# Residue-major layout for dilated attention, output stores from GpSimd's queue and a redone step order in an attention and feed-forward kernel

## The chip, the cores and the metric

The kernel runs on one core of one Trainium2 chip. The metric is the device time of one execution, in microseconds. A profile is taken from one execution of its own, and its span is a little shorter than the time of that execution (324.1 against 325.84 us for the kernel before). An execution is called slow when it takes over 1.5% longer than the fastest of the same kernel; ratios here use fast executions alone.

## The reference

Two stages follow one another: causal sliding attention, whose heads 4 to 7 are dilated by four, and a feed-forward pair with a leaky activation.

```python
B, H, S, D = 8, 8, 576, 64                      # attention; window 32, dilation 4
rel = pos[:, None] - pos[None, :]
mask_plain = (rel >= 0) & (rel < 32)                       # heads 0 to 3
mask_dil   = (rel >= 0) & (rel < 128) & (rel % 4 == 0)     # heads 4 to 7
attn = softmax(where(mask, q @ k.T / sqrt(D), -1e9));  x = attn @ v
x = x.transpose(0, 2, 1, 3).reshape(4608, 512)
h = x @ w_in                     # 512 -> 2048
out = maximum(0.01 * h, h) @ w_out   # 2048 -> 512, float32
```

## The kernel before

Everything is ordered by hand. A string, `PROGRAM`, is a list of steps, and each engine executes its share of them in that order. "Batch" n below is one half of the heads of one of the 8 batches: even n are the plain heads, odd n the dilated ones, so n runs from 0 to 15. A unit u is a third of a batch, n = u // 3.

| step | what it issues |
|---|---|
| `lq:n`, `gq:n`, `lv:n` | loads of q and k (from SyncE's queue, or as fp16 from GpSimd's), and of v |
| `lw:0:g`, `lw:1:g` | load quarter g of w_in, of w_out, from GpSimd's queue |
| `cq`, `cv` | casts of q or k, a copy inside v; the letter names the engine (V, P, A) |
| `T:n`, `B:n:p` | transposes of q and k, by DMA or on TensorE |
| `S:u`, `M:u`, `D:u` | scores and exp; mask; denominator, values and their product into `xT` |
| `I:c:j` | 4 matmuls of x @ w_in for chunk c, column block j; step I:c:j uses quarter j // 4 |
| `O:t:g` | 4 matmuls of g @ w_out for tile t of 128 tokens; after g = 3 the tile is stored |
| `Z:m` | m warm-up matmuls on zeros |

```python
PROGRAM = """
... cq:1:q:V:1 lw:0:0 ... lw:0:1 D:1:lp gq:2:b ... lw:0:2 B:3:1:VA M:5 lw:0:3 B:3:0:VA lv:2:b ...
gq:4:b S:11:m I:0:0 I:0:1 I:0:2 S:10:m ... I:0:7 I:0:8 S:7:m I:0:9 lw:1:2 ...
"""
# ... cut
    def transpose(n):
        for nm, dst in (("q", qT), ("k", kT)):
            o = dst[n % NB][:, -2 * S:].rearrange("p (c r) -> p c r", r=96)
            nc.sync.dma_start_transpose(o, qkh[n, nm][0:96, :])
# ... cut, in scores(u): kind is 1 for the dilated heads
                if kind:
                    ka = kT[n % NB][r, tok - 128 + j: tok - 128 + j + 4 * kp - 3: 4]
                    qa = qT[n % NB][r, tok - PAD + j: tok - PAD + j + 4 * w - 3: 4]
                else:
                    ka = kT[n % NB][r, tok + 96 * j - 32: tok + 96 * j + 96]
                    qa = qT[n % NB][r, tok - PAD + 96 * j: tok - PAD + 96 * j + 96]
                nc.tensor.matmul(sps[0:kp, hh, w * x:w * x + w], ka, qa, ...)
# ... cut
    def ff_out(t, g):
        if g == 0:
            ops[t] = psm.tile([128, 512], FP32, tag="pm", name="op")
        op = ops[t]
        g0 = 128 * t % GRING
        for j in range(4 * g, 4 * g + 4):
            nc.tensor.matmul(op, gt[:, j, g0:g0 + 128], w2[g][:, j % 4, :],
                             start=(j == 0), stop=(j == 15))
        if g == 3:
            ob = moe.tile([128, DM], FP32, tag="ob", bufs=2, name="ob")
            nc.scalar.copy(out=ob, in_=op)
            nc.scalar.dma_start(out[128 * t:128 * t + 128, :], ob)
            del ops[t]
```

The dilated heads read q and k transposed with a step of four columns, `ka` and `qa`. That step is what the first part of the change takes away.

The softmax here doesn't subtract the row's maximum and nothing guards it: scores larger than these inputs give would overflow.

## Time and profile before

| | before |
|---|---|
| time, median of three executions | 325.28 us (324.02 to 325.45) |
| span of the profile | 324.1 us |
| TensorE (PE) busy | 317.0 us, 98% |
| PE idle from 52 to 320 us | 0.00 us |
| step I:0:8 starts | 35.33 us |
| last matmul ends | 320.57 us |

The prediction shows the rows on which its argument rests. Three further rows of the page of the kernel before matter later. The first is the clock granted to PE in 40 equal slices, in tenths. The second counts DMA packets. The third is a group of instructions: line, engine, operation, operands and count, then busy us and mean ns of one, then idle time just before them and what ended most of it.

```profile
PEclk9999999999999999999999999999999999999999
DMA packets 111198, 42.38 MB, mean 131 GB/s; under 512 B 96832, under 2 KB 105024, under 8 KB 111168
...
L334 PE MATMUL hp<-xT,w 128*128 128x384 f16 (+1 forms) x832 | 140.9, 315 | 0.7 <-DMA w<-in_moe_w_in_dram 0.7
```

The clock never falls. All 832 matmuls of the first feed-forward product together waited 0.7 us, all of it for a quarter of w_in. So the start hangs on a load, but very little PE time is lost to it.

### The profile page before, as it was taken

To read this page: it belongs to the slowest core of one execution; us is meant where nothing else is said; L and a number is where in the kernel's file an instruction comes from. 1 tells how busy PE (TensorE), PEld (TensorE's weight loads), DVE (VectorE), ACT (ScalarE), POOL (GpSimd) and SP (SyncE) were. 2 spreads that over 40 slices of the span, in tenths; PEclk is the share of its full clock that TensorE was granted. 3 is DMA by queue.
4 is the path that set the end of the run, shared out by engine and by line. 5 is a ranking of instruction groups with operands and counts; after the bars stand their busy time and mean duration, and the time that the engine had idled before them with its cause. 6 is when DMAs were issued, how large, how long until landed. Compare 5 with 4: busy or idle time off the path is not lost.

```text
span 324.1 us, 6641 instructions
## 1 busy us (share of the span) xinstructions
PE 317.0 (98%) x2805; PEld 185.4 (57%) x2805; DVE 111.2 (34%) x166; ACT 191.8 (59%) x379; POOL 69.3 (21%) x92
## 2 busy tenths in 40 slices
PE   8998999999999999999999999999999999999995
PEld 3565585565756656656555565555665655565542
DVE  3473363203633084012353650454561530040000
ACT  1778696555756765936755773636856754464312
POOL 8751076033054220040310610200150000000000
PEclk9999999999999999999999999999999999999999
DMA  7999999969949931579899869303755000100003
GB/s 230 209 197 196 185 180 176 164 186 106 252 79 288 205 58 48 130 161 163 116 251 245 97 115 238 85 12 117 198 67 77 34 33 28 39 34 32 32 35 129
DMA packets 111198, 42.38 MB, mean 131 GB/s; under 512 B 96832, under 2 KB 105024, under 8 KB 111168
## 3 DMA queue, kind: packets, MB, share of 16 engines
q1 hardware_dynamic: 78240, 21.83, 34.2%
q0 software_dynamic: 27744, 10.68, 28.5%
q10 hardware_dynamic: 5184, 9.44, 7.9%
q8 instruction: 22, 0.36, 0.5%
q14 instruction: 8, 0.07, 0.1%
HBM read 36.70 MB, written 9.44 MB: 142 GB/s over the span
## 4 chain that ended last, share of the span: by engine, by line
PE 88%; DMA 9%; POOL 2%; ACT 0%; issue 0%; POOLq 0%
PE op L344 39%; PE hp L334 38%; DMA w<-in_moe_w_in_dram 5%; PE sps L261 5%; DMA vh<-in_v_dram 4%; PE den L287 3%; PE o L295 2%; PE tp L212 0%; POOL vh L169 0%; POOL vh L198 0%; POOL qh L183 0%; ACT ob L348 0%; POOL bias L106 0%; POOL bias L104 0%; POOL bias L103 0%
## 5 line engine op out<-in xcount | busy, mean ns | idle before, releaser
L334 PE MATMUL hp<-xT,w 128*128 128x384 f16 (+1 forms) x832 | 140.9, 315 | 0.7 <-DMA w<-in_moe_w_in_dram 0.7
L344 PE MATMUL op<-w,gt 128*128 128x512 f16 x576 | 137.0, 379 | 0.0
L336 ACT ACTIVATE gt<-hp 128x384 f16<-128x384 f32 (+1 forms) x208 | 93.0, 465 | 66.2 <-PE hp L334 63.8
L334 PEld LDWEIGHTS <-w 128*128 128x128 f16 x832 | 88.7, 114 | 43.9 <-issue 1.6
L344 PEld LDWEIGHTS <-gt 128*128 128x128 f16 x576 | 55.1, 98 | 57.2 <-issue 0.5
L312 DVE TENSOR_TENSOR xT<-o,rec 128x384 f16<-128x384 f32 (+1 forms) x64 | 33.6, 554 | 108.0 <-ACT rec L301 90.0
L303 DVE RECIPROCAL rec<-den 128x384 f32<-128x384 f32 x14 | 35.8, 2555 | 35.3 <-PE den L287 35.3
L264 ACT ACTIVATE er<-sps 128x768 f16<-128x768 f32 (+1 forms) x48 | 38.6, 804 | 10.7 <-PE sps L261 8.8
L348 ACT COPY ob<-op 128x512 f32<-128x512 f32 x36 | 21.1, 586 | 33.6 <-PE op L344 33.5
L186 POOL CAST kh<-kf 96x768 f16<-96x768 f32 x16 | 14.6, 936 | 106.3 <-DMA kf<-in_k_dram 81.2
L271 DVE TENSOR_TENSOR em<-er,mask 128x768 f16<-128x768 f16 (+1 forms) x44 | 25.4, 600 | 18.0 <-ACT er L264 17.8
L261 PE MATMUL sps<-qT,kT 64*128 64x96 f16 (+1 forms) x448 | 22.9, 229 | 0.0
L300 ACT ACTIVATE ln<-den 128x384 f32<-128x384 f32 x34 | 16.6, 488 | 8.7 <-PE den L287 8.1
L261 PEld LDWEIGHTS <-kT 64*128 64x128 f16 (+1 forms) x448 | 14.9, 121 | 10.2 <-issue 8.6
L301 ACT ACTIVATE rec<-ln 128x384 f32<-128x384 f32 x34 | 17.8, 524 | 1.1
L295 PEld LDWEIGHTS <-vh 128*64 128x64 f16 (+1 forms) x448 | 15.5, 110 | 2.4
L295 PE MATMUL o<-em,vh 128*64 128x96 f16 (+1 forms) x416 | 15.4, 201 | 0.0
L287 PE MATMUL den<-em,ones 128*64 128x384 f16 (+1 forms) x88 | 15.4, 346 | 0.0
L387 PE MATMUL wp<-xT 128*128 128x512 f16 x37 | 12.6, 455 | 1.5 <-DVE xT L113 1.3
L174 POOL DMA_DIRECT2D vh<-in_v_dram x16 | 10.0, 627 | 18.8 <-PE o L295 18.8
L195 POOL COPY vh<-vh 32x1472 f16<-32x1472 f16 x5 | 7.0, 1404 | 24.6 <-DMA vh<-in_v_dram 24.5
L287 PEld LDWEIGHTS <-ones 128*64 128x64 f16 (+1 forms) x96 | 5.3, 107 | 10.0 <-issue 8.3
(51 smaller groups left out, 97.8 us busy)
## 6 DMA issues: line engine op xcount, KB each, us to landing
out_dram<-ob ACTq DMA_DIRECT2D x36, 256.0 KB, 2.2
qf<-in_q_dram SPq DMA_DIRECT2D x11, 576.0 KB, 6.5
kf<-in_k_dram SPq DMA_DIRECT2D x11, 576.0 KB, 7.7
vh<-in_v_dram POOLq DMA_DIRECT2D x8, 288.0 KB, 7.5
w<-in_moe_w_in_dram POOLq DMA_DIRECT2D x4, 512.0 KB, 16.1
w<-in_moe_w_out_dram POOLq DMA_DIRECT2D x4, 512.0 KB, 11.1
vh<-in_v_dram POOLq DMA_DIRECT2D x8, 192.0 KB, 5.6
qf<-in_q_dram SPq DMA_DIRECT2D x4, 288.0 KB, 5.3
```

The lines of the kernel that those rows point to most:

```text
L261: nc.tensor.matmul(sps[0:kp, hh, w * x:w * x + w], ka, qa, start=not pe_mask, stop=not pe_mask or x == len(tiles) - 1)
L264: nc.scalar.activation(out=er[0:kp], in_=sps[0:kp, :, 0:384], func=AF.Exp, scale=SCALE)
L271: nc.vector.tensor_tensor(out=em[0:kp].rearrange("p h (t c) -> p h t c", c=w), in0=er[0:kp].rearrange("p h (t c) -> p h t c", c=w), in1=ba ...
L287: nc.tensor.matmul(den[64 * hh:64 * hh + 64, 0:384], ones[0:kp], em[0:kp, hh, :], start=True, stop=True)
L295: nc.tensor.matmul(o[64 * hh:64 * hh + 64, w * x:w * x + w], vt[0:kp, sl, :], em[0:kp, hh, w * x:w * x + w], start=True, stop=True)
L301: nc.scalar.activation(out=rec, in_=ln, func=AF.Exp, scale=-1.0)
L303: nc.vector.reciprocal(out=rec, in_=den[:, 0:384])
L312: nc.vector.tensor_tensor(out=out_x, in0=ins[0], in1=ins[1], op=ALU.mult)
L334: nc.tensor.matmul(hp[:, 0:w], w1[j // 4][:, i, j % 4::4], xT[:, i, x0:x0 + w], start=(i == 0), stop=(i == 3))
L336: nc.scalar.activation(out=gt[:, j, g0:g0 + w], in_=hp[:, 0:w], func=AF.Prelu, alpha=0.01)
L344: nc.tensor.matmul(op, gt[:, j, g0:g0 + 128], w2[g][:, j % 4, :], start=(j == 0), stop=(j == 15))
L348: nc.scalar.copy(out=ob, in_=op)
```

## The change

The change has five parts.

- **Residue-major**: q and k of the dilated batches 5, 7, ..., 15 are loaded, cast and transposed so that tokens of one residue modulo four are neighbours. The scores then read contiguous columns. It takes two transposes for each of q and k instead of one, four pieces of a cast instead of two, and larger tiles; the fp16 tiles get three buffers instead of four (`QHB`).
- **Stores**: four output buffers instead of two, and tiles 0 to 7 are stored from GpSimd's queue. The change was announced as moving most stores; its code moves 8 of 36.
- **Last tile in halves**: 16 matmuls, copy and store for columns 0 to 255, then the same for 256 to 511, so that the first store overlaps the second half.
- **Order**: the whole list of steps is new. It begins with the dilated batch 1, has 25 warm-up matmuls ahead of I:0:0 for 37, and loads the quarters of w_in as 0, 1, 3, 2.
- **No other arithmetic changes.**

```diff
-QHB = 4
+QHB = 3
 PROGRAM = """
-lq:0:0 Z:2 bias lq:0:1 lq:1:0 lq:1:1 lv:0:b Z:4 cq:0:q:P:0 cq:0:k:V:0 Z:9 lv:1:b B:0:0:AA cq:0:q:P:1
 ... (60 lines cut)
+Z:4 bias Z:3 lq:1:1 gq:3:b lv:1:b lv:0:b Z:2 cq:1:q:V:1 Z:5 gq:2:b lw:0:0 lw:0:1 cq:1:k:A:1 lw:0:3
+lw:0:2 B:1:1:AA lq:1:0 lv:3:b lq:0:0 lq:0:1 Z:2 cq:1:q:A:0 S:4:b cq:1:k:V:0 Z:3 B:1:0:VA cv:1:V:b
 ... (cut)
+D:5:lp S:11:m I:0:0 I:0:1 I:0:2 S:2:m I:0:3 I:0:4 I:0:5 M:2 lv:5:b I:0:6 I:0:7 S:9:m D:2:r I:0:8
 ... (cut)
+    if n >= NPE and n % 2:                                        # in load_qk
+        for a, i0, w in ((0, 0, 96), (1, 96, 48)):
+            nc.sync.dma_start(t[0:w, 16 * a:16 * a + 16, :].rearrange("p (h r) d -> p h (r d)", r=4),
+                              rows_ap(x, ((n // 2 * H + 4) * S + 4 * i0) * D,
+                                      [[4 * D, w], [S * D, 4], [1, 4 * D]]))
 ... (cast and transpose cut: four pieces, two transposes)
+                if kind and n >= NPE:                             # in scores
+                    c = S * p + 144 * j + (96 if s == 2 else 0)
+                    ka = kT[n % NB][r, PAD + c - 32: PAD + c - 32 + kp]
+                    qa = qT[n % NB][r, c: c + w]
 ... (cut)
+        last = t == NTOK // 128 - 1                               # in ff_out
+        if last and g < 3:
+            return
+        for c0, c1 in ((0, 256), (256, 512)) if last else ((0, 512),):
+            for j in range(0 if last else 4 * g, 4 * g + 4):
+                nc.tensor.matmul(op[:, c0:c1], gt[:, j, g0:g0 + 128], w2[j // 4][:, j % 4, c0:c1],
+                                 start=(j == 0), stop=(j == 15))
+            if g == 3:
+                ob = moe.tile([128, DM], FP32, tag="ob", bufs=4, name="ob")
+                nc.scalar.copy(out=ob[:, c0:c1], in_=op[:, c0:c1])
+                queue = nc.gpsimd if t < 8 else nc.scalar
+                queue.dma_start(out[128 * t:128 * t + 128, c0:c1], ob[:, c0:c1])
```

## The prediction

> **What bounds the kernel now.** I read the busy shares first, then the busy time of four stretches, then the chain of waits, then single groups. Page part 1, and the stretches from start to 36, 52, 320 and 325 us (columns: engine, busy us, instructions):
>
> ```profile
> PE 317.0 (98%) x2805; PEld 185.4 (57%) x2805; DVE 111.2 (34%) x166; ACT 191.8 (59%) x379; POOL 69.3 (21%) x92
> ...
> 0.00:36.00 36.00, 32.47 (x525) 17.95 (x525) 18.25 (x38) 22.24 (x38) 18.76 (x34) 1.00 1.18 206
> 36.00:52.00 16.00, 16.00 (x238) 12.17 (x238) 6.61 (x8) 13.43 (x33) 9.55 (x12) 1.00 1.23 186
> 52.00:320.00 268.00, 268.00 (x2047) 155.18 (x2042) 86.37 (x120) 155.59 (x308) 40.98 (x47) 1.00 0.62 118
> ```
>
> PE is busy 268.00 of 268.00 us from 52 us on, while ACT is at 58% and the DMA engines at 0.62. Ends of matmuls are modelled, so I ask the chain of waits (start us, length us, what) whether that is dense issue or long latency:
>
> ```profile
> 5.02 11.97 DMA vh<-in_v_dram
> 17.04 0.98 POOL vh L198
> 18.02 17.26 DMA w<-in_moe_w_in_dram
> 35.33 0.84 PE hp L334 x4
> 36.17 0.28 PE sps L261 x8
> 36.44 6.41 PE hp L334 x48
> ...
> 81.47 0.46 PE sps L261 x7
> 81.92 0.97 PE op L344 x4
> ...
> 83.55 0.71 PE sps L261 x16
> ...
> 167.29 0.97 PE op L344 x4
> ...
> 215.04 4.32 PE op L344 x20
> ```
>
> Here 20 `op` matmuls take 4.32 us, 0.216 each, and in the same view 20 `hp` matmuls take 3.25, 0.163 each: no holes. So there are two regimes. **Up to 35.3 us the chain is DMA**: the third quarter of w_in lands at 18.02+17.26 = 35.28, and step I:0:8, its first user, starts at 35.33. **From there PE itself is the chain**, with only attention between feed-forward matmuls. The last matmul ends at 320.57 (the final `ob` copy starts at 320.61), so PE needs 320.57-35.33 = **285.2 us after I:0:8**; 3.5 us of copy and store follow. Nothing on ACT, DVE, Pool or SP can shorten 285.2; only PE instructions that get cheaper, or an earlier 35.3.
>
> **What the Trainium skill says.** "TensorE: Matmul & The Clock Gate", Back-to-back issue gap, gives N/2.4+2.5 ns, 216 for N=512: the trace agrees (0.216). The same page, Weight-path perf modes, says that the fast weight load wants 128 weight columns: the trace fits it, score weight loads of 128 columns take 94 ns and those of 80 columns 168 (lines below). "Advanced Engine Details and Errata", SBUF Cachelines, wants two hits on a 16-byte line; a step of 4 fp16 values (8 bytes) has them, so by the page the dilated scores should cost nothing extra. The trace differs: eight contiguous score matmuls take 0.28 us of the chain, eight at step 4 take 0.46. I go by the trace. "DMA: Bandwidth & Descriptors", Issuing engines are not separate DMA queues, says that the issuing engine saves only sequencer time: I take that for the stores; no row of before tests it.
>
> The score lines, contiguous (window at 48.7), step 4 (81.3) and the 80x48 blocks (83.4); duration ns min/median/max:
>
> ```profile
> L261 PEld LDWEIGHTS <-kT x8: 92/94/96, 48.7 to 48.8; 64*128 64x128 f16 x8
> L261 PE MATMUL sps<-qT,kT x8: 202/203/213, 48.7 to 48.9; 64*128 64x96 f16 x8
> ...
> L261 PEld LDWEIGHTS <-kT x8: 108/113/132, 81.4 to 81.6; 64*128 64x128 f16 x8
> L261 PE MATMUL sps<-qT,kT x8: 252/264/270, 81.4 to 81.7; 64*128 64x96 f16 x8
> ...
> L261 PEld LDWEIGHTS <-kT x16: 147/168/170, 83.5 to 84.0; 64*80 64x80 f16 x16
> ```
>
> **The change, part by part.**
> 1. *Residue-major layout of dilated q and k (batches 5, 7, ..., 15; 1 and 3 keep step 4).* Six batches with two units of 8 matmuls: 12 x (0.46-0.28) = 2.2 us off PE. Six units of 16 blocks, 0.71 us each: with the step gone, eight pairs would take 0.28 to 0.35 us if the step caused all of it, and some 0.69 if the 80-column weight load is itself the limit. I take the middle, 0.53: 6 x 0.18 = 1.1 us (0.1 to 2.4). Sum **3.3 us on the path**. Around it: loads of 1 KB rows in place of 256 B, four transposes in place of two, four casts in place of two. A 96x768 cast takes 936 ns on Pool and 550 on DVE, both engines far from full; off the path.
> 2. *Order redone.* Each change between feed-forward, scores and values costs PE 0.10 us: `op x4` is 0.97 in the chain above just after attention against 0.86 inside a run. Counting changes in the two step lists from I:0:8 on: 116 before, 105 after, so **1.1 us less**. One score unit, S:10, moves from ahead of I:0:8 to behind it: +0.35.
> 3. *Last tile in halves.* 32 matmuls of 256 columns at about 0.109 instead of 16 at 0.216: +0.05. The last copy shrinks from 128x512 (586 ns) to 128x256; by the slope of the 128x384 and 128x192 `gt` activations (489 and 330 ns) that is 374 ns. The store behind it is half as large (2.0 to 2.2 us to landing now, mostly not size). **0.3 us less** after PE.
> 4. *Stores from Pool's queue, four buffers.* By the diff only tiles 0 to 7 of 36. It takes 8 x 0.338 us of issue off ACT, idle four tenths of the time; the `ob` copies wait for `op` (33.5 us), not for a buffer. Nothing on the path.
>
> From I:0:8 to the last matmul: 285.2-3.3-1.1+0.35+0.05 = **281.2 us**. Tail: 3.5-0.3 = 3.2.
>
> **The start decides the rest.** Pool's queue carries w_in. In the timeline its four loads are issued at 10.61, 13.16, 18.02 and 18.76 and land 14.2 (shortest) to 19.6 us (longest) later, so first at 24.8, last at 38.4. In those 13.6 us it also carries q and k of batch 2: three w blocks of 1.05 MB and 1.18 MB of q, k, 0.32 MB/us of source, 3.3 us a block. Before, I:0:8 needs the third block. After, the order on Pool is quarters 0, 1, **3, 2**, and I:0:8 reads quarter 2: the last block, with q, k of 2 now also ahead of all four. The same bytes lie before the last block as before, so it should land near 35.3+3.3 = 38.6. The loads are issued without Pool work between, but the queue was already full. PE has no more work ahead of I:0:8 than before, so it would reach it near 34 and wait four to five us. Fewer warm-up matmuls (25 for 37 ahead of I:0:0) cost nothing if DMA bounds the start.
>
> **Rivals.**
> - *A: the start is not later.* Something else delayed before's third block, or the first loads overlap better, and I:0:8 starts near 35.3: span 35.3+281.2+3.2 = 319.7. Measured time is 1.2 above the profiled span (325.28 against 324.1): 320.9. For it: before's order had almost no PE holes, so whoever ordered the steps knew this chip, and the new order should fit as well.
> - *B: the last block lands at 38.6:* 38.6+281.2+3.2+1.2 = 324.2. For it: the same bytes and the full DMA queues (1.18 to 1.23 of busy share, overlapping). Batch 6 is prefetched at 256 B rows and batch 5 follows it, one prefetch more than before's single batch 5 in this stretch, which could add one or two us. A hole of five us could also let PE's clock fall back; the warm-up matmuls at the start average 455 ns, not 379.
> - *C: a new wait inside the steady stretch.* Pool now holds its queue for stores, so casts and v loads behind them come later, and transposes wait. Against: Pool is 15% busy from 52 us on, and its `kh` casts wait 81 us for loads already. Each us of PE hole would add a us; I give it 10% for more than 2 us.
> - *D: a much earlier start.* To beat 2% (below 318.8) I:0:8 must start before 33.2 us, or the 80-column blocks must drop fully and the start gain a us. I see no removed byte that buys it.
>
> **Range and chances.** A and B at 0.45 and 0.55 give 0.45 x 320.9 + 0.55 x 324.2 = 322.7. The 80-column blocks swing 1.2 us either way, the start 2: 80% range 319.0 to 326.0. Faster by over 2% needs D: 0.09. Slower by over 2% (above 331.8) needs C badly: 0.03. Within 2%: 0.88.
>
> **What would show each step.** Score units of batches 5 and up at 0.28 us in the chain; 16-block units anywhere from 0.3 to 0.7 (this settles the weight-load question). PE from I:0:8 to the last matmul near 281. A `hp` wait on the DMA of `w` of some four us near 34 to 38 us says B; none says A. Batches 5 and up still at 0.46 would refute part 1; PE holes past 52 us behind `sps` or `vh` say C. The prediction is wrong above all if w's last block lands much before 36 or after 41 us.

## The result

The changed kernel takes 328.78 us (median of four, 327.14 to 329.16) against 325.01 (324.02 to 325.45) in the same rounds. The ratio is 1.0108, with a 95% interval of 1.0072 to 1.0144. Ratios in this document are the mean time of one kernel's fast executions over that of the other's of the same rounds, so not quite the ratio of the medians quoted. The kernel became about 1% slower. That is "same" at the 2% mark, the side that the prediction gave 0.88, but the time lies outside the predicted range of 319.0 to 326.0.

The profiled execution was the fastest one (327.14 us). The page of the changed kernel:

```profile
PE 312.5 (96%) x2811; PEld 186.0 (57%) x2811; DVE 111.4 (34%) x169; ACT 197.3 (61%) x389; POOL 79.8 (25%) x111
...
PEclk9987999999999999999999999999999999999999
...
DMA packets 90670, 42.38 MB, mean 130 GB/s; under 512 B 69776, under 2 KB 85136, under 8 KB 90640
```

PE works 4.5 us less than before (312.5 against 317.0) and the span is 1.3 us longer, so idle time took more than was saved. Not all of the 4.5 us is the layout: twelve warm-up matmuls are gone as well, and work at half clock counts double. The clock falls early on, in slices 3 and 4. There are a fifth fewer packets for the same bytes; the layout alone has as few (91038), so the longer rows of its loads make the difference. Next the same three stretches as before (columns: PE, PEld, DVE, ACT, POOL busy us, then clock, DMA share, GB/s):

```profile
0.00:36.00 36.00, 30.29 (x491) 18.09 (x493) 14.39 (x35) 21.34 (x37) 18.53 (x33) 0.91 1.17 208
36.00:52.00 16.00, 14.49 (x176) 11.04 (x170) 9.63 (x11) 11.57 (x29) 6.62 (x8) 1.00 1.31 225
52.00:320.00 268.00, 265.76 (x2142) 155.36 (x2135) 87.41 (x124) 163.99 (x324) 54.66 (x71) 1.00 0.62 116
```

PE now has 2.24 us of holes from 52 to 320 us, where it had none. (A hole in this document is the idle time that the timeline puts in brackets, unless it says otherwise.) The chain of waits of the changed kernel shows where its start comes from (start us, length us, what):

```profile
4.68 9.61 DMA vh<-in_v_dram
...
14.58 23.66 DMA w<-in_moe_w_in_dram
...
38.28 5.39 PE hp L355 x32
43.67 0.46 PE sps L282 x7
...
46.89 2.57 DVE rec L324
...
50.88 0.65 DVE qh L188
...
51.55 0.89 DVE qh L188 x2
...
53.05 0.33 DVE qh L188
...
53.80 1.56 DVE xT L333 x3
55.36 0.48 DVE em L292
...
55.88 0.35 PE den L308 x2
```

First, I:0:8 starts at 38.28, just after the last quarter of w_in landed at 14.58+23.66 = 38.24. This is rival B of the prediction. Second, the path then runs through VectorE from 46.9 to 55.8 us: a reciprocal, pieces of the cast of batch 5 (`qh`, 1.87 us together), products and a mask, and only then step D:6. PE stood still for 1.30 us in front of it. A cast that was to be off the path is on it.

The timeline of PE in the changed kernel shows the holes themselves; the bracket gives idle time before and what ended it:

```profile
20.63 0.23 PE L316 MATMUL o<-er,vh 128*64 128x96 f16 x1
22.95 0.53 PE L316 MATMUL o<-er,vh 128*64 128x96 f16 x7 [2.09 <-POOL vh L206]
...
36.45 0.34 PE L316 MATMUL o<-em,vh 128*64 128x96 f16 x8
38.28 3.93 PE L355 MATMUL hp<-xT,w 128*128 128x384 f16 x23 [1.50 <-DMA w<-in_moe_w_in_dram]
...
55.88 0.35 PE L308 MATMUL den<-em,ones 128*64 128x384 f16 x2 [1.30 <-DVE em L292]
```

PE waits 2.09 us for a copy inside v, and the records give it half the clock from 22.41 to 29.24 us. That delayed the work ahead of I:0:8, which is why only 1.50 us of hole is left in front of it here.

The score units of batches 5 and up, 16 blocks of 80x48, are the groups below (columns as in the prediction). In the chain such a unit takes 0.42 us, where it took 0.71 before.

```profile
L282 PEld LDWEIGHTS <-kT x16: 109/120/120, 118.5 to 118.8; 64*80 64x80 f16 x16
L282 PE MATMUL sps<-qT,kT x16: 192/193/213, 118.5 to 118.8; 64*80 64x48 f16 x16
...
118.61 0.42 PE sps L282 x16
```

Finally the end of the changed kernel, then that of the kernel before, from the timelines:

```profile
319.59 0.37 ACT L374 COPY ob<-op 128x256 f32<-128x256 f32 x1 [0.97 <-PE op L370]
...
320.01 1.91 PE L370 MATMUL op<-w,gt 128*128 128x256 f16 x16 [0.46 <-ACT ob L374]
321.96 0.37 ACT L374 COPY ob<-op 128x256 f32<-128x256 f32 x1 [2.00 <-PE op L370]
```

```profile
320.61 0.59 ACT L348 COPY ob<-op 128x512 f32<-128x512 f32 x1 [1.82 <-PE op L344]
```

The copy is shorter, 0.37 us for 0.59, but the second half of the matmuls waited until the copy of the first half was done. In the timeline it is ScalarE's copy (`ACT ob`) that ends its idle time of 0.46 us, and in the code both halves are one PSUM tile, `op`. From the last matmul to the end of the span it is 3.52 us, and was 3.57.

### The profile page after: what moved, and what is told of

Its sections match the earlier page's. It is cut to its first block, busy times and chain, and to the rows that moved or that the text cites. A ratio compares the mean times of both kernels' runs of the same rounds, so it can differ in the third digit from the quotient of the medians.

```text
span 325.4 us, 6728 instructions
## 1 busy us (share of the span) xinstructions
PE 312.5 (96%) x2811; PEld 186.0 (57%) x2811; DVE 111.4 (34%) x169; ACT 197.3 (61%) x389; POOL 79.8 (25%) x111
## 4 chain that ended last, share of the span: by engine, by line
PE 81%; DMA 10%; ACT 2%; DVE 2%; issue 2%; POOL 1%; POOLq 0%; DVEq 0%
PE op L370 37%; PE hp L355 36%; DMA w<-in_moe_w_in_dram 7%; PE sps L282 3%; DMA vh<-in_v_dram 3%; PE den L308 3%; PE o L316 2%; DVE rec L324 1%; ACT ln L321 1%; DVE xT L333 1%; ACT er L285 1%; DVE qh L188 1%; ACT rec L322 1%; PE tp L229 0%; DVE em L292 0%
## 5 line engine op out<-in xcount | busy, mean ns | idle before, releaser
L370 PE MATMUL op<-w,gt 128*128 128x512 f16 (+1 forms) x592 | 137.9, 373 | 0.5 <-ACT ob L374 0.5
L370 PEld LDWEIGHTS <-gt 128*128 128x128 f16 x592 | 56.6, 98 | 55.5 <-issue 0.6
L374 ACT COPY ob<-op 128x512 f32<-128x512 f32 (+1 forms) x37 | 21.2, 573 | 34.7 <-PE op L370 32.7
L292 DVE TENSOR_TENSOR em<-er,mask 128x768 f16<-128x768 f16 (+1 forms) x43 | 24.3, 587 | 22.5 <-ACT er L285 22.2
L282 PE MATMUL sps<-qT,kT 64*128 64x96 f16 (+1 forms) x448 | 19.1, 210 | 0.3
L206 POOL COPY vh<-vh 32x1472 f16<-32x1472 f16 x8 | 13.3, 1660 | 24.1 <-DMA vh<-in_v_dram 23.9
L282 PEld LDWEIGHTS <-kT 64*128 64x128 f16 (+1 forms) x448 | 12.4, 106 | 11.5 <-issue 9.1
L178 POOL DMA_DIRECT2D vh<-in_v_dram x16 | 10.1, 638 | 8.8 <-DMA vh<-in_v_dram 4.7
L197 POOL CAST kh<-kf 96x768 f16<-96x768 f32 x8 | 6.7, 879 | 20.6 <-DMA kf<-in_k_dram 20.6
L414 PE MATMUL wp<-xT 128*128 128x512 f16 x25 | 9.3, 480 | 1.5 <-DVE xT L112 1.3
L173 POOL DMA_DIRECT2D vh<-in_v_dram x8 | 9.6, 1204 | 3.9 <-PE hp L355 2.1
```

The costliest lines, as they stand in the source:

```text
L282: nc.tensor.matmul(sps[0:kp, hh, w * x:w * x + w], ka, qa, start=not pe_mask, stop=not pe_mask or x == len(tiles) - 1)
L292: nc.vector.tensor_tensor(out=em[0:kp].rearrange("p h (t c) -> p h t c", c=w), in0=er[0:kp].rearrange("p h (t c) -> p h t c", c=w), in1=ba ...
L370: nc.tensor.matmul(op[:, c0:c1], gt[:, j, g0:g0 + 128], w2[j // 4][:, j % 4, c0:c1], start=(j == 0), stop=(j == 15))
L374: nc.scalar.copy(out=ob[:, c0:c1], in_=op[:, c0:c1])
```

## The experiments

Fifteen kernels ran. All were timed in five rounds against the kernel before on the same chip, all gave correct results, and none changes what is computed. They ran in four calls, each on a chip of its own, so kernels of different calls are compared by their ratios to the kernel before. Each time is a median; "before" is the median of the kernel before in the same call.

**The theory**: exchanging the last two quarters of w_in puts the step I:0:8 behind the last load, and the hole there costs clock as well; the layout itself gains. **The rivals**: the layout costs more around it than it gains; the halves or the stores cost the time; the thin start with few warm-up matmuls is the cause; or the difference is scatter from execution to execution.

### Both kernels once more

`a_again` is the changed kernel and `b_again` the kernel before, without an edit.

> The changed kernel once more, to have a trace of its usual state and a time beside the variants of this group. The first trace was its fastest execution (327.14 us, granted clock 0.99); the others had 0.984 and 328.8. Theory 1 (a late quarter of w_in, holes after it, and a clock that falls in the holes): 328.5 us, ratio to the kernel before 1.011; I:0:8 starts when the last quarter lands, near 38.3 us; the clock is at half for some 10 us in two stretches instead of 6.8 us in one. Theory 2 (clock has no part, the first trace just differs): the extra 1.7 us then shows as PE holes at full clock.

> The kernel before itself, for a second trace. Theory 1 (its start moves by two us between executions with what the DMA engines do first, and PE's stretch after I:0:8 does not): ratio 1.000, I:0:8 between 33 and 36 us. Rival (the variants start earlier because of their edits): I:0:8 at 35.3 again.

The changed kernel took 328.16 us against 324.52, ratio 1.0106 (1.0087 to 1.0124). The kernel before against itself took 324.97 against 324.45, ratio 1.0008 (0.9987 to 1.0028). The loss is real. The second profile of the changed kernel has its clock fall in another place. Stretches of its span around I:0:8, columns as above:

```profile
34.50:38.00 3.50, 0.26 (x10) 0.12 (x6) 3.18 (x3) 0.66 (x1) 0.57 (x1) 1.00 1.22 239
38.00:42.20 4.20, 4.12 (x15) 2.14 (x16) 0.97 (x3) 1.47 (x3) 1.11 (x2) 0.59 1.17 239
42.20:46.00 3.80, 3.80 (x32) 2.57 (x31) 0.47 (x1) 2.77 (x6) 1.42 (x2) 1.00 1.73 216
```

This time PE was idle for 3.3 us ahead of I:0:8 (34.76 to 38.08), and then ran at half clock from 38.75 to 42.17. The four steps I:0:8 to I:0:11 took 4.3 us instead of 2.6, so the hole was followed by a second loss of 1.7 us. The 2.09 us wait for the copy inside v is in this profile too, from 21.00 to 23.09, but here the clock stayed full behind it. The start is where theory 1 had it; of its two slow stretches only one is there. In the executions of the first run the mean granted clock was 0.990 at 327.14 and 328.09 us, and 0.983 to 0.984 at 328.76 to 329.16; the kernel before has 0.998 to 1.000 in all 28 executions of these two tests. Only profiled executions show where in the span the clock fell.

The second profile of the kernel before corrects a reading of the first. Its chain of waits:

```profile
16.71 20.53 DMA w<-in_moe_w_in_dram
37.24 0.05 issue
37.29 4.44 PE hp L334 x36
```

Here the path goes through the fourth quarter, landed at 37.24, and I:0:12, which waited for it, while I:0:8 had started at 33.06. The last matmul ends 282.4 us after I:0:12 (319.67-37.29). In the first profile that is 282.2 (320.57-38.41), and the fourth quarter landed at 38.37 there. In the first trace both of the last quarters arrived just in time, and the prediction saw only the third. So in both traces I:0:12 starts as the *last* quarter lands, and the time from there on is the same. The start itself moves between executions, by 1.1 us here.

### The order of the quarters, in the changed kernel

```diff
- ... lw:0:1 cq:1:k:A:1 lw:0:3 lw:0:2 B:1:1:AA ...
+ ... lw:0:1 cq:1:k:A:1 lw:0:2 lw:0:3 B:1:1:AA ...
```

> The changed kernel with the quarters of w_in loaded in order 0,1,2,3 instead of 0,1,3,2. Theory 1 (I:0:8 is held by the block that lands last): quarter 2 lands one block earlier, near 34.5 us, I:0:8 to I:0:11 (2.6 us) run before quarter 3 is there, so 2 to 3 us less than the changed kernel, 325.5 to 326.5. Rival (the late start is hidden because PE is in any case behind, by D:0 and the slow clock): under 0.7 us.

It took 325.42 us against 324.52, ratio 1.0031 (0.9998 to 1.0065): 2.7 us of the loss go by this one exchange (2.4 us by the ratios), near the four steps of 0.65 us that it puts ahead of the last landing. Its executions spread from 323.39 us, with the clock at 1.000, to 327.38, with 0.988. The profiled one (327.05 us, clock 0.979) ran at half clock from 14.44 to 24.68 and from 55.40 to 58.81, the latter after PE had waited 1.93 us for a mask, ahead of D:6. So the exchange is the largest single part of the loss, and the other holes of the new order account for at least some of the rest.

### The order of the quarters, in the kernel before

```diff
- lw:0:2 B:3:1:VA M:5 lw:0:3 B:3:0:VA
+ lw:0:3 B:3:1:VA M:5 lw:0:2 B:3:0:VA
```

> The kernel before with only quarters 2 and 3 of w_in exchanged in the loading order. Theory 1 (the block that lands last holds I:0:8): I:0:8 starts near 38.4 instead of 35.3 and PE then idles for some 4 us ahead of it, after which its clock is at half for 3.4 us: 2.6 to 3 us for the wait and up to 1.7 for the clock, 327 to 329. Rival (the start has slack): within 0.7 us of before.

It took 329.72 us against 324.45, ratio 1.0154 (1.0128 to 1.0181). This exchange alone costs 5.0 us by the ratio, more than the whole change does and more than the 327 to 329 us expected. A second kernel fills the hole with warm-up matmuls, to separate waiting from clock:

```diff
- I:0:7 I:0:8
+ I:0:7 Z:15 I:0:8
```

> The kernel before with quarters 2 and 3 exchanged, and 15 warm-up matmuls (3.2 us) in the hole that this makes ahead of I:0:8. Theory 1 (of the 5.2 us that the exchange costs, the wait is some 3.3 and the fallen clock some 1.8): clock 1.0 from 6 us on, 3.2 to 3.7 us more than before, 327.8 to 328.2. Rival (the clock does not matter, all of it is the wait): 5 us more as without warm-ups, 329.7.

It took 327.92 us against 324.73, ratio 1.0101 (1.0072 to 1.0131). The stretches around I:0:8, without and then with the warm-up matmuls:

```profile
32.50:36.90 4.40, 0.39 (x3) 0.01 (x1) 0.88 (x2) 0.50 (x2) 0.00 (x0) 0.90 1.44 177
36.90:42.80 5.90, 5.87 (x25) 2.71 (x26) 0.56 (x1) 2.23 (x4) 2.88 (x4) 0.50 1.40 202
```

```profile
32.50:36.60 4.10, 3.74 (x19) 1.58 (x16) 1.00 (x2) 0.62 (x2) 0.00 (x0) 1.00 1.41 178
36.60:42.20 5.60, 5.58 (x40) 3.78 (x41) 0.56 (x1) 3.94 (x8) 2.57 (x3) 1.00 1.45 202
```

I:0:8 starts at nearly the same time, 36.93 and 36.62, in both when its quarter has landed. Behind it the clock is 0.50 in one and 1.00 in the other: in 5.9 us at half clock PE gets 25 matmuls done, in 5.6 us at full clock 40. Five of the six executions with the warm-up matmuls have a mean clock of 1.000, and the six without have 0.990 to 0.995. By the ratios, the exchange costs 1.01% (3.3 us) as a wait and another 0.53% (1.7 us, by the two intervals 0.4 to 3.0) as clock. The wait fits the steps that come to stand behind the last landing: in the first trace of the kernel before, I:0:8 to I:0:11 with a score unit between them take 3.1 us (35.33 to 38.41). Rival B of the prediction had 3.3 us for the wait; the clock it named and did not price.

### Warm-up matmuls in the changed kernel

```diff
- B:1:0:VA cv:1:V:b B:3:0:VA ... B:3:1:VV D:0:l ... D:2:r I:0:8
+ B:1:0:VA cv:1:V:b Z:4 B:3:0:VA ... B:3:1:VV Z:9 D:0:l ... D:2:r Z:7 I:0:8
```

> The changed kernel with 20 more warm-up matmuls in the three long holes of the start (4 ahead of B:3:0, 9 ahead of D:0, 7 ahead of I:0:8). Theory 1 (the holes let the clock fall, and in most executions the slow clock reaches work that bounds): granted clock 1.0 throughout from 6 us on, 1 to 2 us less than the changed kernel, 327. Rival (the start is bound by DMA, the clock does not matter): within 0.3 us.

It took 328.43 us against 324.52, ratio 1.0121 (1.0105 to 1.0136), and so missed. Two of the three fillers did what they should: the trace has full clock until 38.0. The third failed because a warm-up matmul writes the tile `den`, which step D:2 just ahead was still reading for its reciprocal. The seven matmuls came late, from 38 to 41 us, at half clock, and pushed I:0:8 to 40.92. So the run does not show what any of the three fillers is worth. It bears on the clock all the same: the slow stretch, from 38.00 to 41.41 us, fell almost wholly on warm-up matmuls, and from I:0:8 to the last matmul this kernel needs 282.8 us, where the second profile of the changed kernel needs 284.5.

### The last tile

```diff
-        last = t == NTOK // 128 - 1
+        last = False
```

> The changed kernel with the last tile computed and stored whole, as before. Theory 1 (the second half waits on ACT's copy of the first, 0.62 us of hole, and the store is not faster): 0.5 us less than the changed kernel. Rival (halving does help the tail, as predicted): 0.3 us more.

The changed kernel with its last tile whole took 326.79 us against 324.52, ratio 1.0065 (1.0053 to 1.0078). Halving therefore cost 1.4 us by the medians. The kernel before with the halves alone:

> The kernel before with the last tile in halves alone. Theory 1 (second half waits for ACT's copy of the first): a hole of 0.6 us between the halves, 0.3 us saved in copy and store, so 0.3 to 0.5 us more than before. Rival (halving helps as predicted, the hole belongs to the new order): 0.2 to 0.3 us less.

It took 325.09 us against 324.45, ratio 1.0020 (0.9994 to 1.0045), and the wait between the halves is in its timeline too:

```profile
317.79 1.91 PE L349 MATMUL op<-w,gt 128*128 128x256 f16 x16 [0.53 <-ACT ob L353]
```

In the changed kernel the tail behind the last matmul is 3.76 us with the tile whole and 3.52 with halves, so halving saves 0.24 there; in the kernel before it is 3.57 and 3.48. The matmuls lose 0.62 by the wait (from start to start, the step between the halves takes 0.73 us instead of 0.11) and 0.05 by their number. The traces thus account for some 0.4 us of loss, 0.6 in the kernel before. That the medians of the changed kernel differ by more is not explained. Its executions with the tile whole are within 0.8 us of one another although their mean clock runs from 0.982 to 1.000, so a fallen clock does not cost the same wherever it falls.

### The stores

```diff
-            nc.scalar.dma_start(out[128 * t:128 * t + 128, :], ob)
+            queue = nc.gpsimd if t < 8 else nc.scalar      # and four buffers
+            queue.dma_start(...)
```

> The kernel before with stores of tiles 0 to 7 from Pool's queue and four output buffers alone. Theory 1 (stores are off the path): within 0.4 us of before. Rival (Pool holds its queue behind the stores, casts and loads come late): holes ahead of sps or tp between 60 and 110 us, over 1 us more.

It took 325.05 us against 324.45, ratio 1.0014 (0.9987 to 1.0040): nothing.

### The layout alone

This is the kernel before, in its own order, with the new load, cast, transpose and scores (four fp16 buffers as before).

```diff
+                if kind and n >= NPE:      # and the load, cast and transpose of the change
+                    ka = kT[n % NB][r, PAD + c - 32: PAD + c - 32 + kp]
+                    qa = qT[n % NB][r, c: c + w]
```

> The kernel before with the residue-major layout of dilated q and k alone (loads, casts, transposes, scores of batches 5 to 15), old step order, four half buffers. Theory 1 (PE is the chain from I:0:8 on, so cheaper score matmuls come off the end one for one): per unit 0.46 to 0.28 us and, as the trace of the changed kernel has it, 0.72 to 0.42 for the 16-block units, 12 x 0.18 + 6 x 0.30 = 4.0 us less, 320.5, ratio 0.988. Rival (more DMA packets, casts and transposes come back as holes): under 2 us less, holes ahead of sps of odd batches.

It took 322.09 us against 324.45, ratio 0.9936 (0.9904 to 0.9967). The layout gains, but less than the 4.0 us that the score units promise. PE's busy time from I:0:8 to the last matmul, before and with the layout, shows 3.5 us:

```profile
35.33:320.57 285.24, 285.24 (x2284) 167.78 (x2284) 92.98 (x128) 169.02 (x340) 50.53 (x58) 1.00 0.66 122
...
32.80:316.53 283.73, 281.72 (x2286) 164.90 (x2283) 94.05 (x138) 169.56 (x345) 55.15 (x70) 1.00 0.69 122
```

And PE has 2.01 us of holes there, where it had none. The largest is one which the timeline explains:

```profile
66.90 0.58 ACT L375 COPY ob<-op 128x512 f32<-128x512 f32 x1 [4.18 <-DMA out_dram<-ob]
67.53 1.72 PE L356 MATMUL hp<-xT,w 128*128 128x384 f16 x8 [1.45 <-ACT ob L375]
```

ScalarE waited 4.18 us for an output buffer whose store was still under way, and PE waited for ScalarE. With two buffers, a store that takes longer while the new loads run holds up the matmuls. So I added one:

```diff
-            ob = moe.tile([128, DM], FP32, tag="ob", bufs=2, name="ob")
+            ob = moe.tile([128, DM], FP32, tag="ob", bufs=3, name="ob")    # ln: one buffer
```

> The kernel before with the residue-major layout and three output buffers instead of two (the scratch ln in one buffer to make room). In the trace with two buffers PE stood 1.8 us at 66 us: the output copy on ACT waited 4.2 us for an earlier store that was slow beside the new loads. Theory 1 (the missing 1.6 us of the 4.0 expected are such waits, most of it this one): that hole is gone, 1.5 us less than with two buffers, 320.6. Rival (another wait takes its place): within 0.5 us of it, 322.

Four output buffers and four fp16 buffers do not fit together: the build refuses them, with 6 KB a partition left where 8 are needed, and even three need `ln` cut to one. With three fp16 buffers it builds. That may be why the change has three; no run tests what they cost. It took 321.37 us against 324.73, ratio 0.9893 (0.9858 to 0.9929). One execution of 325.93 us counts as slow and is left out of the ratio; without it the median is 320.92. Its mean clock was 0.988, so it is of the kind that the changed kernel has all the time. **It beats both kernels.** Its stretch up to 316 us:

```profile
52.00:316.00 264.00, 263.06 (x2023) 151.36 (x2021) 85.78 (x127) 154.71 (x310) 42.51 (x52) 1.00 0.62 118
```

PE has 0.94 us of holes left there, the hole at 66 us is gone, and the clock stays up. So extra output buffers are not idle ballast, as the prediction took them to be: with the new layout a third one removes a wait. What that is worth is not clear of the noise: 0.9893 against 0.9936 is 1.4 us, as theory 1 had it, but the two intervals overlap and come from different chips. Nor is all of the gain on the kernel before the layout's: from I:0:12 to the last matmul this profile takes 279.56 us against 282.16 and 282.39, 2.6 to 2.8 less, and it also starts I:0:12 earlier, at 36.07 against 38.41 and 37.29, in a part that the edit does not touch. Two casts on ScalarE stood near the smaller holes of the layout alone. Moving them to GpSimd was tried on top:

```diff
- cq:9:q:A:b ... cq:15:k:A:b
+ cq:9:q:P:b ... cq:15:k:P:b
```

> The same, with the two odd-batch casts that ACT does (q of 9, k of 15, now four pieces each) moved to Pool. Theory 1 (pieces on ACT hold back the activations that free PE's buffers; 0.4 us of hole at 130 us): 0.3 to 0.6 us less than c_res3. Rival (Pool brings them too late, holes ahead of sps): the same or more.

It took 321.33 us (321.16 without one slow execution), ratio 0.9889 (0.9865 to 0.9913): no difference to the kernel without it. Its trace has holes of 0.88, 0.62 and 0.27 us in other places instead.

### Repairing the changed kernel

All suspected costs of the new order were taken away together: quarters in order, the last tile whole, the two early fillers of warm-up matmuls, and the cast of q of batch 5 moved behind the masks that D:6 and D:7 wait for.

```diff
- cq:5:q:V:b I:1:12 ... cq:5:k:P:b T:5 lq:7:b I:1:15 M:6 O:0:1 M:7
+ I:1:12 ... cq:5:k:P:b I:1:15 M:6 O:0:1 M:7 cq:5:q:V:b T:5 lq:7:b
```

> The changed kernel repaired at the places that the traces name: quarters in order, last tile whole, 4 and 9 warm-ups in the two early holes, the four cast pieces of q of batch 5 on DVE behind the two mask products that D:6 and D:7 wait for. Theory 1: 2.7 us less for the quarters, 1.0 for the tile, 0.7 to 2 for the hole ahead of D:6 and the clock that falls in it: 322 to 324, below the kernel before. Rival (the order as such is bad in the steady stretch): above 325.

It took 324.67 us against 324.73, ratio 0.9980 (0.9951 to 1.0010). That is between the two expectations: the loss is gone and the gain is not there. The profiled execution has full clock throughout and I:0:8 at 34.84, but a new hole of 1.7 us ahead of S:25, which waits for the transpose of k of batch 8:

```profile
153.48 0.34 PE L240 MATMUL sps<-qT,kT 64*128 64x96 f16 x8 [1.67 <-DMA kT<-kh]
```

Nothing in the trace ties that transpose to the moved cast of batch 5, and the changed kernel has no hole there. The repaired order still takes 2.8 us more, by the ratios, than the old order with the same layout and three output buffers. Their profiles show where: from I:0:8 to the last matmul PE stands for 3.36 us here (1.67 in the line above, 0.60 at 37.6 us for the last quarter, 0.64 at D:6 and D:7) against 0.88 there, and I:0:8 starts 1.8 us later. Why the new order leaves these holes, and whether the later start is more than scatter, is not shown.

### Two single repairs

One moves the load of q and k of batch 2 behind the first two quarters of w_in, with the quarters in order.

```diff
- gq:2:b lw:0:0 lw:0:1 cq:1:k:A:1 lw:0:3 lw:0:2
+ lw:0:0 lw:0:1 gq:2:b cq:1:k:A:1 lw:0:2 lw:0:3
```

> The changed kernel with quarters in order and q, k of batch 2 loaded behind quarter 1 as before, not ahead of quarter 0. Theory 1 (order of blocks in Pool's queue is all): quarters 0 and 1 land 3.7 us earlier than with quarters in order alone, near 24 and 27.5, but quarters 2 and 3 not; B:2:0 and D:1 stand ahead of I:0:0 on PE and wait for batch 2, so the end moves by under 0.7 us either way from that kernel's 325.4. Rival (batch 2's place costs the start a part of its own): 1 us or more less, 324.4 or below.

It took 331.17 us against 324.45, ratio 1.0213 (1.0190 to 1.0236), and the expectation missed. In the new order B:2:0 and B:2:1, which need batch 2, stand ahead of I:0:0 on PE, and PE waited 4.49 us for q and 1.14 for k of batch 2. Its stretch up to 38.2 us, in which I:0:0 started at 35.13, is at half clock from end to end:

```profile
24.60:38.20 13.60, 7.98 (x127) 5.56 (x127) 2.18 (x4) 5.61 (x11) 4.83 (x9) 0.50 1.22 205
```

The other moves the cast of batch 5 alone, with the diff shown above for the repair.

> The changed kernel with only the four cast pieces of q of batch 5 on DVE moved behind the mask products of units 6 and 7. Theory 1 (they hold DVE while D:6 waits on its mask product): hole ahead of D:6 under 0.3 us instead of 0.7 to 1.5, 0.5 to 1 us less than the changed kernel, 327.5. Rival (D:6 waits for ACT's exponential, not for DVE): unchanged, 328.2.

It took 328.16 us against 324.45, ratio 1.0104 (1.0077 to 1.0131), unchanged. The hole ahead of D:6 did shrink, to 0.14 us after 1.30 and 0.50 in the two profiles of the changed kernel. But its profiled execution had the clock at half from 37.5 to 44.4 and PE came to D:6 1.5 to 2.1 us later than in the changed kernel, which leaves VectorE more time. Two kernels in which the cast stayed where it was, the last tile whole and batch 2 loaded later, have 0.15 and 0.14 us there too. So the chain of the changed kernel shows the cast on the path, but neither that it alone caused the hole nor what the hole cost is shown.

## Why the prediction was wrong

**What bounds the kernel: right in kind, one step short.** Up to some 38 us a load is the path, then PE is. The prediction took the third quarter for the bound, from a single trace. The second trace shows the fourth, by way of I:0:12. This strengthens rival B: if the last landing sets the pace, then the question is only how many steps stand behind it. Exchanging the quarters puts four more behind it, at 0.65 us each (2.6 us, against the 2.4 to 2.7 that putting them back saves in the changed kernel).

**The steps that failed: the stretch after I:0:8, and the weight of rival A.** "From there PE itself is the chain" made the stretch from I:0:8 to the last matmul a sum of PE instructions at full clock, 281.2 us. The two profiles have 283.6 and 284.5. In the first, other engines held PE up (2.24 us of holes); in the second, half clock behind the hole at I:0:8 cost 1.7 us and holes 1.08. The smaller failure is "A and B at 0.45 and 0.55", which took 1.5 us off for a start at 35.3 that the list of loads argued against. B was right to 0.6 us: the quarter landed at 38.24 and 38.03, where 38.6 was predicted. With B alone the prediction would have read 324.2, still 4.0 to 4.6 us short.

**The clock: named, not priced.** "A hole of five us could also let PE's clock fall back" stands in rival B without a number. The pair of kernels with and without matmuls in that hole puts 1.7 us on it (0.4 to 3.0). The claim that fewer warm-up matmuls "cost nothing if DMA bounds the start" was not tested alone. The changed kernel has early holes and half clock which the kernel before doesn't, and where these fell it shifted the waiting rather than the start: I:0:8 began within 0.2 us in both profiles, behind the same load.

**The layout: right, one term too small.** 12 units at 0.18 us came as predicted. The 16-block units saved 0.30 each instead of 0.18, so 4.0 us in all instead of 3.3. PE's busy time from I:0:8 on shows a little less, 3.5 to 3.8 us (below). The 80-column weight load fell from 168 to 120 ns without its step, so the step was the greater part of the limit.

**"Off the path": wrong.** The casts are in four pieces, and the chain of the changed kernel runs through all four of q of batch 5 on VectorE. Rival C gave 10% to more than 2 us of holes in the steady stretch; there are 2.24 us of them in the first profile and 1.08 in the second. Most of them came from VectorE's order (1.30 us) and the last tile (0.46), not from GpSimd's queue, as rival C had it.

**The last tile: wrong sign.** -0.3 and +0.05 became -0.24 (-0.09 in the kernel before) and +0.67, since the halves share a PSUM tile and the second waits for the copy of the first.

**The stores: right** for the queue (1.0014, with 8 of 36 stores moved), as "DMA: Bandwidth & Descriptors", Issuing engines are not separate DMA queues, has it. The statement that no buffer is waited for held for the kernel before, and stopped holding once the layout changed the traffic (4.18 us in the kernel with the layout alone).

**The new order: right in sign, too large.** No run changes the order alone, but the profiles allow an estimate. PE's busy time from I:0:8 to the last matmul is 285.24 and 285.45 us in the kernel before, 281.72 and 281.68 with the layout in the old order, and in the changed kernel:

```profile
38.28:321.92 283.64, 281.37 (x2308) 167.43 (x2308) 95.41 (x134) 174.37 (x350) 61.27 (x78) 1.00 0.65 121
```

The changed kernel also does S:10 there, which its chain shows at 0.46 us and not 0.35 (batch 3 keeps the step of four), and 0.05 more for the halves. So the fewer changes between kinds of matmul bring 0.8 us instead of 1.1 (0.7 in the repaired kernel, 281.47 us), and the layout 3.5 to 3.8. Busy times are modelled at the ends, so this stays an estimate.

**The time outside the span.** 1.2 us were added, the difference between a median and the span of another execution. The profiled execution itself was 1.74 us longer than its span.

Starting from B's 324.2 us, the second profile adds up so: -0.5 for the start, +3.3 from I:0:8 to the last matmul, +0.3 for the tail and +0.5 for the time outside the span give 327.8; this execution took 327.87. The first gives 324.2 - 0.3 + 2.4 + 0.3 + 0.5 = 327.1, and took 327.14. The medians, 328.16 and 328.78, are higher; most of the slower executions have a lower mean clock (0.984), and no profile of one was kept.

Taken the other way, the parts done alone in the kernel before are -1.07% (layout with a third output buffer), +1.54% (quarters), +0.20% (halves) and +0.14% (stores), together +0.8%; the whole is +1.06% to +1.08%. That the two are near does not show that the parts add up: undone in the changed kernel, the exchange is worth 0.75% and the halves 0.41%, not 1.54% and 0.20%. **Where the gain went**: the layout did take 3.5 to 3.8 us off PE. The exchange of two loads took 2.4 to 2.7 us back and the halves 1.3 to 1.4. Some 3 us more went to holes and a later start of the new order, which no single repair brought back; the cause of those stays open.

## What to carry to other kernels

Where a load sets the start, ask which step waits for the *last* piece and how much work stands behind it; loading pieces in another order than they are used cost that work here once as waiting (3.3 us) and, as PE stood still, a second time as clock (1.7 us). Look at two traces before naming the wait that binds, as two loads that arrive just in time look like one. When a layout is improved, change the layout first, alone, in the order that already fits; then look for the buffer or cast that its new traffic has made late, here the output buffer, and only then redo the order.

## What the Trainium skill lacked or had wrong

- "Advanced Engine Details and Errata", SBUF Cachelines: two hits on a 16-byte line should do. A step of four fp16 values has two, and yet eight score matmuls took 0.46 us instead of 0.28, and 16 blocks 0.71 instead of 0.42, which is 4.0 us of this kernel by the score units and 3.5 to 3.8 by PE's busy time.
- "TensorE: Matmul & The Clock Gate", Weight-path perf modes: the fast load wants 128 columns, and the prediction read the 168 ns of the 80-column loads partly in that light, beside 94 ns for contiguous loads of 128. At the same step 128 columns took 113 ns. Without the step the 80-column loads took 120 ns, and a load with its matmul went by in 0.42/16 = 26 ns. The page does not mention what a stepped read costs here.
- The same page, HAM oscillation: it warns of idle gaps over about 3.4 us, and the table at its end of about 3. Here a hole of 3.3 us ahead of I:0:8 was followed by half clock for 3.4 us, but so were waits of 2.1 us (half clock for 6.8 us in the first profile of the changed kernel) and 1.9 us (for 3.4 us, behind D:6 with the quarters in order). The same wait of 2.1 us left the clock full in the second profile, so the length of one hole alone does not decide it. The slow stretches lasted 3.4, 6.8, 10.2 and 13.6 us, one to four of the page's windows of 3413 ns. The hole that the exchange makes in the kernel before cost 1.7 us beyond the wait.
- "TensorEngine Tiling (Array Packing)" says that changing the tiling mode drains the engine, but no page has the price of changing between full-array feed-forward matmuls and 64-row or 64-column attention matmuls. Here four `op` matmuls took 0.97 us just after attention and 0.86 inside a run.
- "TensorE: Matmul & The Clock Gate", Back-to-back issue gap, from which the prediction took its 216 ns: the section calls the formula that of an isolated matmul and gives about 131 ns for N = 512 in a stream of weight loads and matmuls. Here 20 `op` matmuls in such a stream took 4.32 us, 216 ns each, so the formula holds for the stream and the 131 ns do not.
